# A new hand-searched order, nine check buffers and small operations shared with GpSimd in a three-stage fp32 kernel

## The chip, the cores and the metric

One Trainium2 chip, one core of it. Five engines of the core run their own instruction streams: TensorE (PE in the profile; PEld is its weight load, which runs beside the matmuls), VectorE (DVE), ScalarE (ACT), GpSimd (POOL) and SyncE (SP), which issues all data transfers (DMAs) of this kernel. The metric is the device time of one execution in microseconds (us), the median of several runs.

## The reference

The kernel computes three stages, in float32 with the weights of the two MoE stages given as float64 words:

```python
# attention: B=2, H=8, S=768, D=64; 8 global keys and a local window of 96
scores = q @ k.T / sqrt(D) - slope[h] * dist      # kept where (key < 8) or (0 <= row - key < 96)
a = softmax(scores); x = a @ v                    # x becomes [1536, 512]
# MoE 1: w_in [512, 2048], w_out [2048, 512]
h = x @ w_in
P = a[0] + a[1]*h + a[2]*h**2 + a[3]*h**3
Q = 1 + abs(b[0])*abs(h) + abs(b[1])*h**2
x = (P / (Q + 1e-6)) @ w_out
# MoE 2: w2_in [512, 1024], w2_out [1024, 512]
h = x @ w2_in
s = h * softmax(h)
out = ((s - mean(s)) / sqrt(var(s) + 1e-6) * g_ln) @ w2_out
```

## The kernel before

**Numbers.** Matmuls run on fp32r operands. Each operand is split into a high part (a cast) and a low part (the subtraction value - high, `minus`, L249), and each product is three matmuls: high by high, high by low, low by high. A weight tile comes in as 128x1024 32-bit words (the float64 pairs). The first loads use both words: L892, L896 and L900 on DVE put them together to 128x512 floats, L856/L858/L860 cast the high part (ACT, DVE or POOL) and L249 makes the low part (POOL, or DVE where the tile's number is in `WDVE`).

**Stages.** First, attention: 128-row tiles of queries, 64-wide heads, with PE L748/L751 for the scores, DVE L757 for mask, bias and maximum, ACT L765 for the exponential, PE L781 for the transposes and L788/L800 for the product with v. MoE 1 starts while attention still runs: 64 steps (four segments of 384 rows of x, the first of them done in two parts, by 16 slices of w_in), each with 12 matmuls L989, L991, L995, an elementwise chain on ACT and DVE (L1018 to L1038, of which L1021 is the step's first DVE reading of the matmuls' result and L1034, L1036, L1038 the later ones), and a split into g high and g low (L249 again, on DVE or POOL by the string `GLX`); then 12 matmuls L1086 or 9 of the 512-wide form L1088. MoE 2 has 12 tiles of 128 rows: 24 matmuls L1214 to L1216 (two halves of 512 columns), then the softmax and layer norm of `p2_soft` (DVE maximum L1236 and its negative L1237; ACT exponential L1261; DVE L1240 to L1243; ACT squares L1263; DVE variance L1247; ACT root L1250/1251; a Newton step of four 128x1 operations L1254 to L1257 and the scaling L1258 on DVE), transposes L1277 on PE with casts L1287 (lh) and low parts L249 (ll), 24 matmuls L1302 to L1304, a copy L1313 and the output DMA L1315.

**The weight check.** Words of float64 that are out of the fast path's range must be noticed. In the MoE 2 stage every weight tile is loaded a second time (48 loads of 512 KB, L959 on SP) into one of three buffers in the tile `t`, and DVE L957 ands its high words into `cv`. At the end `w_verdict` halves `cv` nine times (L967) and makes one number per row (L969 to L971), PE L1432 adds the rows, and DVE L224 to L229 turn it into the integer `fi`. All engines load `fi` (L1613); `tc.If` (L1614) then runs a slow path, which these inputs never take.

**What sets the order.** `record` (L557) lists some 2,100 operations, each with engine, modelled duration and the values it reads and writes. `Plan.follow` (L485) replays them in the order of the table `ORDER`, a permutation found by a search under the model; a tile of a pool goes to whichever operation comes next. Strings name the engine of each copy, cast or subtraction (A = ACT, D = DVE, P = POOL). Where the model sees PE idle for long, `fill` (L541) issues 128x128 matmuls on `warm` or `ident` (L544) into a free bank, whose result nobody reads.

```python
            if fill and e == "PE" and gap > (WARM[1] if t < WARM[0] else FILL[0]):
```

Of the kernel before, what the change touches and what calls it, by code (L numbers as in the profile page):

```python
# [1678 lines left out]
```

## Time and profile before

| | |
|---|---|
| time of three runs | 527.73, 529.74, 530.30 us; median 529.74 |
| the profiled execution | 534.36 us, its span 532.6 us |
| PE, PEld, DVE, ACT, POOL busy | 515.1, 448.0, 438.1, 324.3, 129.8 us |
| moved by DMA | 80.92 MB, 152 GB/s on average |

The span runs from the first to the last instruction of the profiled execution; 1.76 us of that execution lie outside it. The stretches of the span, by what PE works on: to about 24 us the start of attention with PE often waiting; to 48 us attention beside the first steps of MoE 1; to 204 us attention and MoE 1 together, ending at the L1021 of step 28; to 354 us MoE 1 alone; to 520 us MoE 2; the rest is the end. The row of a stretch gives each engine's busy time, the clock granted to TensorE (1.00 is 2.4 GHz, 0.50 is 1.2 GHz), the busy share of the DMA engines and what they moved.

### The profile page before, as it was taken

Reading aid. Unit: us, or ns where it says so; the run is one execution under the profiler, and the core shown is the slowest. Engines: PE = TensorE matmul, PEld = TensorE weight load, DVE = VectorE, ACT = ScalarE, POOL = GpSimd, SP = SyncE. Lnnn points to the kernel's source line nnn. Section 1 sums busy time; section 2 is a strip of 40 time slices with the busy share of each in tenths; the row PEclk is TensorE's granted clock in tenths of the full one; section 3 lists DMA queues with packets and bytes.
Section 4 is the critical chain, followed back from the end, with each engine's and each line's share of the span. In section 5 each row is a group of like instructions: output and inputs, shape, how many; then the busy total and the mean of one; then the engine's idle time right before and its main releaser. Section 6 shows DMA issues by size and latency. Waiting matters only on the chain.

```text
span 532.6 us, 9523 instructions
## 1 busy us (share of the span) xinstructions
PE 515.1 (97%) x3294; PEld 448.0 (84%) x3294; DVE 438.1 (82%) x1041; ACT 324.3 (61%) x751; POOL 129.8 (24%) x142
## 2 busy tenths in 40 slices
PE   8998989999999999999999999999999999999995
PEld 6776768887988878999999999998887888888885
DVE  4688999999898997967898999988779777879623
ACT  5577777887768698657666686667255342543310
POOL 3211335664534110013021124453333000000000
PEclk9998999999999999999999999999999999999998
DMA  6579765335672546300233224132344557778781
GB/s 193 172 221 306 237 205 168 124 107 158 197 231 68 164 145 192 92 0 1 69 106 108 90 75 128 42 104 95 118 139 156 165 180 234 240 232 246 263 258 50
DMA packets 37559, 80.92 MB, mean 152 GB/s; under 512 B 4864, under 2 KB 21504, under 8 KB 37504
## 3 DMA queue, kind: packets, MB, share of 16 engines
q1 hardware_dynamic: 37504, 80.24, 48.7%
q8 instruction: 28, 0.46, 0.4%
q14 instruction: 27, 0.22, 0.1%
HBM read 72.36 MB, written 7.86 MB: 151 GB/s over the span
## 4 chain that ended last, share of the span: by engine, by line
PE 58%; DVE 25%; ACT 6%; DMA 5%; issue 3%; SPq 1%; DVEq 0%; ACTq 0%
PE pb L1086 8%; PE pb L1088 5%; PE pb L1302 4%; PE pb L1303 4%; PE pb L1304 4%; PE pb L995 4%; PE pb L989 4%; PE pb L991 4%; PE pb L1214 3%; PE pb L1216 3%; PE pb L1215 3%; DVE cv L896 3%; DVE t L1034 3%; DVE t L1038 3%; PE pb L751 2%
## 5 line engine op out<-in xcount | busy, mean ns | idle before, releaser
L989 PE MATMUL pb<-x,w 128*128 128x384 f32 x256 | 88.3, 345 | 0.2
L991 PE MATMUL pb<-x,w 128*128 128x384 f32 x256 | 86.2, 337 | 0.0
L1088 PE MATMUL pb<-w,g 128*128 128x512 f32 x288 | 71.9, 398 | 0.6 <-DVE g L249 0.6
L1086 PE MATMUL pb<-g,w 128*128 128x384 f32 x384 | 69.8, 335 | 1.3 <-DVE g L249 1.3
L249 POOL TENSOR_TENSOR g<-t,g 128x384 fp32r<-128x384 f32 x37 | 41.0, 1112 | 122.1 <-ACT g L856 50.0
L1086 PEld LDWEIGHTS pb<-g,w 128*128 128x128 f32 x384 | 66.6, 188 | 2.4 <-DVE g L249 2.3
L1088 PEld LDWEIGHTS pb<-w,g 128*128 128x128 f32 x288 | 52.5, 188 | 12.4 <-DVE g L249 1.0
L249 POOL TENSOR_TENSOR w<-wst,w 128x512 fp32r<-128x512 f32 x35 | 47.9, 1374 | 38.5 <-ACT w L856 29.1
L995 PE MATMUL pb<-x,w 128*128 128x384 f32 x256 | 54.1, 337 | 0.0
L1020 ACT ACTIVATE t<-pb,poly 128x384 f32<-128x384 f32 x64 | 36.6, 579 | 24.0 <-PE pb L995 18.2
L1018 ACT ACTIVATE t<-pb,poly 128x384 f32<-128x384 f32 x64 | 42.3, 666 | 14.0 <-PE pb L995 10.2
L989 PEld LDWEIGHTS pb<-x,w 128*128 128x128 f32 x256 | 48.5, 190 | 2.4 <-DVE t L1021 0.8
L991 PEld LDWEIGHTS pb<-x,w 128*128 128x128 f32 x256 | 48.5, 190 | 0.1
L765 ACT ACTIVATE e<-e,st 128x192 f32<-128x192 f32 (+1 forms) x96 | 41.9, 439 | 8.7 <-DVE st L757 8.3
L995 PEld LDWEIGHTS pb<-x,w 128*128 128x128 f32 x256 | 44.9, 188 | 0.5 <-issue 0.3
L1021 DVE SCALAR_TENSOR_TENSOR t<-t,poly,pb 128x384 f32<-128x384 f32 x64 | 38.6, 606 | 6.6 <-ACT t L1018 3.3
L957 DVE SCALAR_TENSOR_TENSOR cv<-t,cv 128x512 int32<-128x512 int32 x47 | 32.7, 695 | 10.8 <-DMA t<-in_w_out 7.5
L1024 ACT ACTIVATE t<-t,poly 128x384 f32<-128x384 f32 x51 | 31.2, 614 | 14.2 <-DVE t L1036 6.7
L1302 PE MATMUL pb<-w,lh 128*128 128x512 f32 (+1 forms) x104 | 39.5, 380 | 0.2 <-ACT wst L1313 0.2
L1303 PE MATMUL pb<-w,lh 128*128 128x512 f32 (+1 forms) x104 | 39.1, 376 | 0.0
L1304 PE MATMUL pb<-w,ll 128*128 128x512 f32 (+1 forms) x104 | 38.8, 373 | 0.0
L1214 PE MATMUL pb<-w,yh 128*128 128x512 f32 x96 | 38.1, 397 | 0.0
(178 smaller groups left out, 1083.1 us busy)
## 6 DMA issues: line engine op xcount, KB each, us to landing
wst<-in_w_in SPq DMA_DIRECT2D x24, 512.0 KB, 4.2
wst<-in_w_out SPq DMA_DIRECT2D x24, 512.0 KB, 4.4
t<-in_w_in SPq DMA_DIRECT2D x24, 512.0 KB, 4.1
t<-in_w_out SPq DMA_DIRECT2D x24, 512.0 KB, 4.5
v<-in_qkv SPq DMA_DIRECT2D x80, 96.0 KB, 3.5
qk<-in_qkv SPq DMA_DIRECT2D x40, 192.0 KB, 3.2
out<-wst SPq DMA_DIRECT2D x11, 256.0 KB, 3.6
x_d<-x SPq DMA_DIRECT2D x2, 768.0 KB, 5.4
```

What stands on the lines that cost most here:

```text
L249: eng.tensor_tensor(out=out, in0=a, in1=hi.bitcast(F32), op=ALU.subtract)
L765: act.activation(out=x, in_=x, func=AF.Exp, scale=-1.0, bias=st[:, 0, c:c + 1], accum_out=st[:, 1, c:c + 1])
L989: pe.matmul(out=pb[:, g.h.slot, 0:n], lhsT=wt[wh.slot][:, cs[p]], rhs=xt[x[0].slot][:, p, 0:n], start=(p == 0), stop=False)
L991: pe.matmul(out=pb[:, g.h.slot, 0:n], lhsT=wt[wl.slot][:, cs[p]], rhs=xt[x[0].slot][:, p, 0:n], start=False, stop=False)
L995: pe.matmul(out=pb[:, g.h.slot, 0:n], lhsT=wt[wh.slot][:, cs[p]], rhs=xt[x[1].slot][:, p, 0:n], start=False, stop=(p == 3))
L1018: op("ACT", 0.2 + 0.467 * k, lambda: act.activation(out=T(g.c), in_=h(), func=AF.Square, scale=poly[:, 0:1], bias=poly[:, 1:2]), r=[g.h, v ...
L1086: pe.matmul(out=pb[:, y[i].slot, 0:n], lhsT=wt[w.slot][:, c], rhs=gt[a.slot][:, 0:n], **k)
L1088: pe.matmul(out=pb[:, y[i].slot, :], lhsT=gt[a.slot][:, c], rhs=wt[w.slot], **k)
L1214: pe.matmul(out=dst, lhsT=yh[:, m, :], rhs=wh, start=(m == 0), stop=False)
L1302: pe.matmul(out=pb[:, b.slot, c], lhsT=lh[:, f, :], rhs=wh[:, c], start=(f == 0), stop=False)
L1303: pe.matmul(out=pb[:, b.slot, c], lhsT=lh[:, f, :], rhs=wl[:, c], start=False, stop=False)
L1304: pe.matmul(out=pb[:, b.slot, c], lhsT=ll[:, f, :], rhs=wh[:, c], start=False, stop=(f == 7))
```

## The change

The table `ORDER` and all engine strings are new, found again by the search under a changed model: PE begins at 1.0 instead of 2.0 us, PE operations before 8 us are taken as 85% longer (`COLD`), and every transfer issued after 2 us as 0.9 us longer (`LATE`). Fillers before 8 us are 256 wide where two fit.

The x tiles of MoE 1 move to a pool of their own (`xp`). After their last use (`switch_x`) the space holds six more buffers for the weight check, so that loads go round over nine; loads into the six wait only for the weights' joins, no longer for the last g splits.

`w_verdict` has three instructions in place of twelve. In `p2_soft` the 128x1 operations become operations of their own, on DVE or POOL by `MNX`, `NGX`, `VRX`, `NWX`; on POOL the Newton step is six instructions. The two halves of the last output tile get a buffer each. `Flag.numbers` and `Flag.factors` take an engine (both stay on DVE), with three maxima in place of one reduction.

```diff
-GLX = 'DPPPPPPPPPDPDPPDPDDPDPDDPPPPDDDPPPDPDDPDDDDDDPPDDPPPDPDPPPPDPPDP'
+GLX = 'PPPPPPPPDPPPPPPPPPPDPPDDPDPDPPDDDDDPDPDDDPPDDDDDDDPDDPDPPDPPPDPD'
-YEX = "A" * 14
-XCX = "D" * 4
-WGX = "P" * 8
-XHX = "A" * 12
-YHX = "A" * 12
-LHX = "A" * 24
-OTX = "A" * 13
-WDVE = (7, 11, 18, 30, 31, 32, 34, 35, 36, 37, 38, 39, 43)
+YEX = 'AAAADADAAAADAD'
+XCX = 'AAPA'
+WGX = 'AAADDPAA'
+XHX = 'AAAAAAAAAAAD'
+YHX = 'DAADADAAAAAD'
+LHX = 'AAAADDAAADDADADAAADDDADA'
+OTX = 'AADDDAAAAAAAA'
+VRX = 'PPPPDPPDPDPD'
+NGX = 'DDDDDPDPDPPD'
+MNX = 'PDDPDDPDDPPD'
+NWX = 'PPPPDPPPPDPP'
+FLX = 'DD'
+WDVE = (4, 6, 9, 10, 20, 22, 23, 27, 28, 29, 30, 31, 32, 33, 34, 36, 39, 40, 41, 42, 43, 45, 47)
...
-BEGIN = {"PE": 2.0, "ACT": 2.5, "DVE": 1.0, "POOL": 1.0, "SP": 1.2, "X": 0.0}
+BEGIN = {"PE": 1.0, "ACT": 2.5, "DVE": 1.0, "POOL": 1.0, "SP": 1.2, "X": 0.0}
...
-                if idle <= BEGIN["PE"]:
-                    fill(int((gap + 1.0) / 0.5), spare, True)
+                if idle < COLD[0]:
+                    n = int((gap + WARM[2]) / 0.46)
+                    fill(n // 2, spare, 256)
+                    fill(n % 2, spare, 128)
...
-        st, first = Val("ck"), nseen[0] == 0
+        in_x, first = nseen[0] % 9 > 2, nseen[0] == 0
+        st = Val("ckx") if in_x else Val("ck")
...
-        w = 256
-        while w:
-            dve.tensor_tensor(out=a[:, 0:w], in0=a[:, 0:w], in1=a[:, w:2 * w], op=ALU.bitwise_and)
-            w //= 2
-        dve.tensor_scalar(out=a[:, 0:1], in0=a[:, 0:1], scalar1=0x78000000, scalar2=None, op0=ALU.bitwise_and)
-        dve.tensor_copy(bad, a[:, 0:1])
-        dve.tensor_scalar(out=bad, in0=bad, scalar1=float(0x78000000), scalar2=None, op0=ALU.not_equal)
+        dve.tensor_scalar(out=a, in0=a, scalar1=0x78000000, scalar2=None, op0=ALU.bitwise_and)
+        dve.tensor_reduce(out=bad, in_=a, op=ALU.min, axis=mybir.AxisListType.X)
+        dve.tensor_scalar(out=bad, in0=bad, scalar1=float(0x78000000), scalar2=None, op0=ALU.is_lt)
...
+    def switch_x():
+        held.pop(0).__exit__(None, None, None)
+        cm = tc.tile_pool(name="cp", bufs=1, side="right")
+        cp = cm.__enter__()
+        held.insert(0, cm)
+        bpt["ck"] = [cp.tile([128, 1024], I32, name=f"ck{i}") for i in range(6)]
...
+                pool.tensor_tensor(out=S(13), in0=S(12), in1=S(12), op=ALU.mult)
+                pool.tensor_tensor(out=S(13), in0=S(13), in1=S(11), op=ALU.mult)
+                pool.tensor_tensor(out=S(13), in0=S(13), in1=S(12), op=ALU.mult)
+                pool.tensor_scalar(out=S(13), in0=S(13), scalar1=-0.5, scalar2=None, op0=ALU.mult)
+                pool.tensor_scalar(out=S(12), in0=S(12), scalar1=1.5, scalar2=None, op0=ALU.mult)
+                pool.tensor_tensor(out=S(12), in0=S(12), in1=S(13), op=ALU.add)
```

DVE at the end of the program, before: the last look at the check's loads (L957), the verdict and the flag.

```order
L249 TENSOR_TENSOR ll_2746<-pb,lh_2744 128x512
L957 SCALAR_TENSOR_TENSOR cv<-t,cv 128x512 x6
L967 TENSOR_TENSOR cv<-cv 128x256
L967 TENSOR_TENSOR cv<-cv 128x128
...
L970 CAST bad<-cv 128x1
L971 TENSOR_SCALAR bad<-bad 128x1
L224 TENSOR_TENSOR fl<-fl,pb 128x1
L228 TENSOR_SCALAR fl<-fl 128x1
L229 CAST fi<-fl 128x1
```

DVE at the same place, after: L975 is the look at the check's loads, L983 to L985 the verdict, L1334 and L259 the last tile's lh and ll.

```order
L975 SCALAR_TENSOR_TENSOR cv<-t,cv 128x512
L983 TENSOR_SCALAR cv<-cv 128x512
L984 TENSOR_REDUCE bad<-cv 128x1
L985 TENSOR_SCALAR bad<-bad 128x1
L1334 CAST lh_2643<-pb 128x512
L216 TENSOR_TENSOR am<-coef 128x4
...
L259 TENSOR_TENSOR ll_2645<-pb,lh_2643 128x512 x2
L234 TENSOR_TENSOR fl<-fl,pb 128x1
L238 TENSOR_SCALAR fl<-fl 128x1
L239 CAST fi<-fl 128x1
```

The verdict stood behind the last tile's work on DVE and stands ahead of it now, with 19 operations of `factors` between the last cast and the last two low parts.

PE at the end, before (L1304 is the last output matmul, L544 the fillers, L1432 the count):

```order
L1303 MATMUL pb<-w_118,lh_2744 128x256
L1304 MATMUL pb<-w_119,ll_2746 128x256
L544 MATMUL pb<-ident 128x128 x26
L1432 MATMUL pb<-bad,t 128x1
L1613 TENSOR_LOAD fi
```

PE at the end, after:

```order
L1350 MATMUL pb<-w_127,lh_2643 128x256
L1351 MATMUL pb<-w_128,ll_2645 128x256
L1484 MATMUL pb<-bad,t 128x1
L1665 TENSOR_LOAD fi
```

The count now follows the last output matmul with no filler between them.

SP's queue at the end, before, with L959 the check's loads and L1315 the outputs:

```order
L1315 DMA out<-wst_157 128x512
L959 DMA t<-in_w_out 128x1024 x4
L1315 DMA out<-wst_155 128x256
L1315 DMA out<-wst_154 128x512
L1315 DMA out<-wst_155 128x256
```

SP's queue at the end, after:

```order
L1362 DMA out<-wst_161 128x512
L977 DMA t<-in_w_out 128x1024 x2
L1362 DMA out<-wst_164 128x512
L1362 DMA out<-wst_161 128x512
L1362 DMA out<-wst_163 128x512
L1362 DMA out<-wst_164 128x512
L1362 DMA out<-wst_161 128x256
L1362 DMA out<-wst_162 128x256
```

The last check load stood ahead of three outputs and stands ahead of six.

## Rows read from the trace of the kernel before

**Rows 1.** The page, first part: span, then busy time of each engine.

```profile
span 532.6 us, 9523 instructions
PE 515.1 (97%) x3294; PEld 448.0 (84%) x3294; DVE 438.1 (82%) x1041; ACT 324.3 (61%) x751; POOL 129.8 (24%) x142
```

**Rows 2.** Stretches: us, PE, PEld, DVE, ACT, POOL busy, PEclk, DMA share, GB/s.

```profile
0.00:24.00 24.00, 21.91 (x121) 16.79 (x123) 12.70 (x57) 12.29 (x44) 7.23 (x23) 1.00 0.62 182
24.00:48.00 24.00, 20.90 (x262) 15.82 (x262) 19.58 (x79) 18.01 (x57) 3.23 (x4) 1.00 0.83 242
48.00:51.50 3.50, 3.50 (x16) 3.07 (x15) 3.31 (x10) 3.18 (x12) 1.25 (x1) 0.51 0.99 356
51.50:125.00 73.50, 71.57 (x485) 59.87 (x484) 71.41 (x157) 56.52 (x129) 34.10 (x30) 1.00 0.57 177
125.00:204.00 79.00, 77.66 (x617) 64.34 (x616) 71.17 (x184) 63.32 (x168) 27.53 (x26) 1.00 0.53 156
204.00:354.00 150.00, 148.44 (x942) 143.71 (x941) 130.95 (x251) 102.17 (x204) 34.55 (x38) 1.00 0.27 81
354.00:520.00 166.00, 165.06 (x811) 138.40 (x810) 124.06 (x290) 68.18 (x140) 21.68 (x20) 1.00 0.60 189
520.00:532.60 12.60, 6.08 (x56) 5.99 (x54) 4.96 (x18) 0.65 (x2) 0.21 (x1) 0.87 0.14 50
```

**Rows 3.** The chain that ended last, by engine.

```profile
PE 58%; DVE 25%; ACT 6%; DMA 5%; issue 3%; SPq 1%; DVEq 0%; ACTq 0%
```

**Rows 4.** The waits of PE: waited for, total us, times, longest.

```profile
PE pb L751 <- DVE t L1021: 2.4, 3, 1.6
PE pb L1086 <- DVE g L249: 1.3, 2, 0.7
```

**Rows 5.** Timeline around a wait of attention's scores: start, duration, instruction.

```profile
47.82 0.70 PE L751 MATMUL pb<-qk 64*64 64x192 f32 x4 [1.59 <-DVE t L1021]
```

**Rows 6.** Timeline of the end.

```profile
519.87 0.28 PE L1304 MATMUL pb<-w,ll 128*128 128x256 f32 x1
519.99 5.97 PE L544 MATMUL pb<-ident 128*128 128x128 f32 x52
520.24 0.65 ACT L1313 COPY wst<-pb 128x256 f32<-128x256 f32 x2 [6.06 <-PE pb L1304]
520.63 1.31 SPq L1315 DMA_DIRECT2D out<-wst  x3
522.34 2.23 DVE L967 TENSOR_TENSOR cv<-cv 128x256 int32<-128x256 int32 x9
525.69 0.30 PEld L1432 LDWEIGHTS pb<-bad,t 128*128 128x128 f32 x2
526.49 0.15 DVE L229 CAST fi<-fl 128x1 int32<-128x1 f32 x1
```

**Rows 7.** DMA issues: count, KB each, median us from issue to landing.

```profile
out<-wst SPq DMA_DIRECT2D x2, 128.0 KB, 1.9
```

**Rows 8.** Groups by line: busy us, mean ns of one, idle before.

```profile
L249 POOL TENSOR_TENSOR w<-wst,w 128x512 fp32r<-128x512 f32 x35 | 47.9, 1374 | 38.5 <-ACT w L856 29.1 <-DVE w L858 8.9
L249 POOL TENSOR_TENSOR g<-t,g 128x384 fp32r<-128x384 f32 x37 | 41.0, 1112 | 122.1 <-ACT g L856 50.0 <-PE pb L1086 34.0 <-PE pb L991 11.5
L249 DVE TENSOR_TENSOR g<-t,g 128x384 fp32r<-128x384 f32 x27 | 15.6, 579 | 0.5 <-PE pb L1086 0.2
L1237 DVE TENSOR_SCALAR st<-st 128x1 f32<-128x1 f32 x12 | 1.8, 154 | 0.4
```

**Rows 9.** Timeline of a MoE 2 tile, from Newton step to transposes.

```profile
395.49 1.22 DVE L1255 SCALAR_TENSOR_TENSOR st<-st 128x1 f32<-128x1 f32 x1
397.12 0.81 DVE L1258 TENSOR_SCALAR wst<-wst,st 128x1024 f32<-128x1024 f32 x1
402.56 0.60 PE L1277 MATMUL pb<-ident,wst 128*128 128x128 f32 x4
```

**Rows 10.** Timeline of attention's first transposes.

```profile
13.12 1.11 PE L781 MATMUL pb<-ident,e 128*128 128x128 f32 x4
```

More of the change, by code (lines that the diff above doesn't have):

```diff
@@ L188, in __init__, with numbers @@
         self.fi = pool.tile([128, 1], I32, name="fi")
-    def numbers(self):
-        dve, nf, neg, nv, fl = self.nc.vector, self.nf, self.neg, self.nv, self.fl
+    def numbers(self, dve):
+        nf, neg, nv, fl = self.nf, self.neg, self.nv, self.fl
         dve.tensor_scalar(out=neg, in0=nf[:, :, 0], scalar1=0.0, scalar2=None, op0=ALU.is_lt)
@@ L200, in numbers, with factors @@
         dve.tensor_tensor(out=fl[:, 0:1], in0=fl[:, 0:1], in1=fl[:, 1:2], op=ALU.max)
-    def factors(self):
-        dve, coef, am, fl = self.nc.vector, self.coef, self.am, self.fl
+    def factors(self, dve):
+        coef, am, fl = self.coef, self.am, self.fl
         dve.tensor_tensor(out=am, in0=coef[:, 0:4], in1=coef[:, 0:4], op=ALU.mult)
-        dve.tensor_reduce(out=fl[:, 1:2], in_=am, op=ALU.max, axis=mybir.AxisListType.X)
+        for i in range(3):
+            dve.tensor_tensor(out=fl[:, 1:2], in0=fl[:, 1:2] if i else am[:, 0:1], in1=am[:, i + 1:i + 2], op=ALU.max)
         dve.tensor_tensor(out=fl[:, 1:2], in0=fl[:, 1:2], in1=am[:, 3:4], op=ALU.mult)
@@ L505, in follow @@
             if e == "PE":
-                wait, was = ENTER[was][o.cls], o.cls
+                wait, was = ENTER[was][o.cls] + (COLD[1] * o.occ if t < COLD[0] else 0.0), o.cls
             o.start, at[e], o.end = t, t + o.occ + wait, t + o.lat + wait
@@ L511, in follow @@
                 dma = max(dma, at[e]) + o.move
-                o.end = dma + o.lat
+                o.end = dma + o.lat + (LATE[1] if t > LATE[0] else 0.0)
             for v in o.vals:
@@ L538, in fast_path, with fill @@
     plan, held = record(tc, es, const, qkv, w_in, w_out, w2_in, w2_out, coef, ab2, g2, ident, flag, out)
-    def fill(n, spare, early=False):
+    def fill(n, spare, early=0):
         for _ in range(n if spare else 0):
-            x = warm if early else ident
-            nc.tensor.matmul(out=plan.pb[:, spare[0], 0:128], lhsT=x, rhs=x, start=True, stop=True)
+            o, x = plan.pb[:, spare[0], 0:max(early, 128)].rearrange("p (a c) -> p a c", c=128), warm if early else ident
+            o, r = bass.broadcast_tensor_aps(o, x.rearrange("p (a c) -> p a c", a=1))
+            nc.tensor.matmul(out=o, lhsT=x, rhs=r, start=True, stop=True)
     with tc.manual_schedule():
@@ L560, in record @@
     abt, ab, g_sb, g_ln = ab2[0], ab2[1], g2[0], g2[1]
+    xp_cm = tc.tile_pool(name="xp", bufs=1, side="right")
+    xp = xp_cm.__enter__()
+    xt = [xp.tile([128, 4, NMAX], F32R, name=f"x{i}") for i in range(4)]
     mp = es.enter_context(tc.tile_pool(name="mp", bufs=1))
@@ L574, in record @@
     gt = [mp.tile([128, NMAX], F32R, name=f"g{i}") for i in range(GB)]
-    xt = [mp.tile([128, 4, NMAX], F32R, name=f"x{i}") for i in range(4)]
     yt = [mp.tile([128, 512], F32, name=f"y{i}") for i in range(YB)]
@@ L587, in record @@
               "t": range(TB), "g": range(GB), "x": range(4), "y": range(YB), "qk": range(QB), "v": range(VB),
[L588 removed]
+              "e": range(EB), "st": range(3), "cv": [0], "ck": range(3), "ckx": range(6), "st2": range(3), "yh": [0, 1], "yl": [0, 1],
               "lh": [0, 1], "ll": [0, 1]})
@@ L949, in words @@
         def words():
+            if in_x:
+                return bpt["ck"][st.slot]
             return tall.rearrange("p a c -> p (a c)")[:, st.slot * 1024:st.slot * 1024 + 1024].bitcast(I32)
@@ L957, in seen @@
                 dve.scalar_tensor_tensor(out=a, in0=w1, scalar=0x40000000, in1=a, op0=ALU.bitwise_xor, op1=ALU.bitwise_and)
-        op("SP", 2.0, lambda: sync.dma_start(out=words(), in_=src.bitcast(I32)), occ=0.43, new=[st], move=2.1, after=gl[-4:] + joins[-1:], tag="ckl")
+        op("SP", 2.0, lambda: sync.dma_start(out=words(), in_=src.bitcast(I32)), occ=0.43, r=[vsx] if in_x else [], new=[st], move=2.1, after=joins[-1:] if in_x else gl[-4:] + joins[-1:], tag="ckl")
         op("DVE", 0.682, seen, r=[st], **{"new" if first else "w": [vacc]}, tag="ck")
@@ L1229, in E @@
         def E():
-            return wst[e.slot].bitcast(F32)
+            return wst[ev.slot].bitcast(F32)
         def S(a):
@@ L1236, in smax, with of, mneg @@
             dve.tensor_reduce(out=S(0), in_=H(), op=ALU.max, axis=mybir.AxisListType.X)
-            dve.tensor_scalar(out=S(2), in0=S(0), scalar1=-1.0, scalar2=None, op0=ALU.mult)
+        def of(x):
+            return "POOL" if x == "P" else "DVE", pool if x == "P" else dve
+        def mneg(eng):
+            eng.tensor_scalar(out=S(2), in0=S(0), scalar1=-1.0, scalar2=None, op0=ALU.mult)
         def times():
@@ L1242, in times, with neg, var @@
             dve.scalar_tensor_tensor(out=E(), in0=H(), scalar=S(6), in1=E(), op0=ALU.mult, op1=ALU.mult, accum_out=S(7))
-            dve.tensor_scalar(out=S(9), in0=S(7), scalar1=-1.0 / DFF2, scalar2=None, op0=ALU.mult)
-        def var():
-            dve.tensor_scalar(out=S(11), in0=S(10), scalar1=1.0 / DFF2, scalar2=1e-6, op0=ALU.mult, op1=ALU.add)
+        def neg(eng):
+            eng.tensor_scalar(out=S(9), in0=S(7), scalar1=-1.0 / DFF2, scalar2=None, op0=ALU.mult)
+        def var(eng):
+            eng.tensor_scalar(out=S(11), in0=S(10), scalar1=1.0 / DFF2, scalar2=1e-6, op0=ALU.mult, op1=ALU.add)
         def root():
@@ L1251, in root, with small @@
             act.activation(out=S(12), in_=S(12), func=AF.Exp, scale=-0.5)
+        def small(eng):
+            if eng is dve:
+                dve.tensor_tensor(out=S(13), in0=S(12), in1=S(12), op=ALU.mult)
+                dve.scalar_tensor_tensor(out=S(13), in0=S(13), scalar=S(11), in1=S(12), op0=ALU.mult, op1=ALU.mult)
+                dve.scalar_tensor_tensor(out=S(12), in0=S(12), scalar=3.0, in1=S(13), op0=ALU.mult, op1=ALU.subtract)
+                dve.tensor_scalar(out=S(12), in0=S(12), scalar1=0.5, scalar2=None, op0=ALU.mult)
+            else:
+                pool.tensor_tensor(out=S(13), in0=S(12), in1=S(12), op=ALU.mult)
[4 more added lines that the diff above has]
+                pool.tensor_tensor(out=S(12), in0=S(12), in1=S(13), op=ALU.add)
@@ L1253, in newton @@
         def newton():
-            dve.tensor_tensor(out=S(13), in0=S(12), in1=S(12), op=ALU.mult)
-            dve.scalar_tensor_tensor(out=S(13), in0=S(13), scalar=S(11), in1=S(12), op0=ALU.mult, op1=ALU.mult)
-            dve.scalar_tensor_tensor(out=S(12), in0=S(12), scalar=3.0, in1=S(13), op0=ALU.mult, op1=ALU.subtract)
-            dve.tensor_scalar(out=S(12), in0=S(12), scalar1=0.5, scalar2=None, op0=ALU.mult)
             dve.tensor_scalar(out=E(), in0=E(), scalar1=S(9), scalar2=S(12), op0=ALU.add, op1=ALU.mult)
-        op("DVE", 1.407, smax, r=o.h, new=[st], tag="max2")
@@ L1261, in p2_soft @@
-        op("ACT", 1.205, lambda: act.activation(out=E(), in_=H(), func=AF.Exp, bias=S(2), accum_out=S(3)), r=o.h, w=[st], new=[e], tag="exp2")
-        op("DVE", 1.86, times, r=o.h, w=[st, e], tag="times")
-        op("ACT", 1.245, lambda: act.activation(out=H(), in_=E(), func=AF.Square, bias=S(9), accum_out=S(10)), r=[e], w=o.h + [st], tag="sq2")
-        op("DVE", 0.15, var, w=[st], tag="var")
+        k = o.k
+        op("DVE", 1.25, smax, r=o.h, new=[st], tag="max2")
+        e, n = of(MNX[k])
@@ new lines, in p2_soft @@
+        op(e, 0.2 if n is pool else 0.15, lambda n=n: mneg(n), w=[st], tag="mneg" if n is dve else "mnegP")
+        op("ACT", 1.205, lambda: act.activation(out=E(), in_=H(), func=AF.Exp, bias=S(2), accum_out=S(3)), r=o.h, w=[st], new=[ev], tag="exp2")
+        op("DVE", 1.7, times, r=o.h, w=[st, ev], tag="times")
+        e, n = of(NGX[k])
+        op(e, 0.2 if n is pool else 0.15, lambda n=n: neg(n), w=[st], tag="neg" if n is dve else "negP")
+        op("ACT", 1.245, lambda: act.activation(out=H(), in_=E(), func=AF.Square, bias=S(9), accum_out=S(10)), r=[ev], w=o.h + [st], tag="sq2")
@@ L1265, in p2_soft @@
+        e, n = of(VRX[k])
+        op(e, 0.2 if n is pool else 0.15, lambda n=n: var(n), w=[st], tag="var" if n is dve else "varP")
         op("ACT", 0.437, root, w=[st], tag="root")
-        op("DVE", 1.642, newton, w=[st, e], tag="newton")
+        e, n = of(NWX[k])
+        op(e, 1.2 if n is pool else 0.83, lambda n=n: small(n), w=[st], tag="nws" if n is dve else "nwsP")
+        op("DVE", 0.82, newton, r=[st], w=[ev], tag="newton")
     def p2_tr(o):
@@ L1295, in p2_o @@
         w = 512 // n
-        b, ot = Val("y2"), Val("wst", "ot")
+        b, ots = Val("y2"), [Val("wst", "ot") for _ in range(n)]
         def mm(c):
@@ L1309, in p2_o @@
                     **{"w" if i else "new": [b]}, occ=5.505 / n + (0.13 if n > 1 else 0.0), tag="o") for i, c in enumerate(cs)]
-        for i, c in enumerate(cs):
+        for i, (c, ot) in enumerate(zip(cs, ots)):
             e = OTX[o.k + i]
             copy = act.copy if e == "A" else dve.tensor_copy
-            op("ACT" if e == "A" else "DVE", (0.585 if n == 1 else 0.372) + (0.0 if e == "A" else 0.1), lambda c=c, copy=copy: copy(wst[ot.slot].bitcast(F32)[:, c], pb[:, b.slot, c]), r=[b],
-               **{"w" if i else "new": [ot]}, tag="ot" if e == "A" else "otD")
-            op("SP", 2.0, lambda c=c: sync.dma_start(out=out[rows, c], in_=wst[ot.slot].bitcast(F32)[:, c]), occ=0.4, r=[ot], move=1.0, tag="out")
+            op("ACT" if e == "A" else "DVE", (0.585 if n == 1 else 0.372) + (0.0 if e == "A" else 0.1), lambda c=c, copy=copy, ot=ot: copy(wst[ot.slot].bitcast(F32)[:, c], pb[:, b.slot, c]), r=[b],
+               new=[ot], tag="ot" if e == "A" else "otD")
+            op("SP", 2.0, lambda c=c, ot=ot: sync.dma_start(out=out[rows, c], in_=wst[ot.slot].bitcast(F32)[:, c]), occ=0.4, r=[ot], move=1.0, tag="out")
     steps = [(si, f) for si, (j, f0, f1) in enumerate(SEGS) for f in range(f0, f1)]
@@ L1410, in record @@
             made2 += 1
+    op("X", 0.0, switch_x, w=[vsx], after=[o for o in P.ops if any(v.pool == "x" for v in o.vals)])
     vflag = Val()
@@ L1422, in record @@
         if k in (6, 8):
-            part_, d = (flag.numbers, 1.38) if k == 6 else (flag.factors, 3.43)
-            op("DVE", d, part_, r=[vnn, vpoly], w=[vflag], after=[fr[k].op], tag="flag")
+            part_, d = (flag.numbers, 1.38) if k == 6 else (flag.factors, 3.45)
+            x = FLX[k // 8]
+            op("POOL" if x == "P" else "DVE", d * (1.3 if x == "P" else 1.0), lambda part_=part_, x=x: part_(pool if x == "P" else dve), r=[vnn, vpoly], w=[vflag],
+               after=[fr[k].op], tag="flP" if x == "P" else "fl")
+            if not wide and k == 8:
+                op("DVE", 0.3, flag.integer, w=[vflag], tag="flag")
         if wide and 1 <= k <= 8:
@@ L1429, in record @@
             bank = Val("h")
-            op("DVE", 2.8, w_verdict, w=[vacc, vbad], tag="flag")
+            op("DVE", 1.3, w_verdict, w=[vacc, vbad], tag="flag")
             op("POOL", 0.3, lambda: pool.memset(ones, 1.0), r=[vacc], w=[vones], tag="ck")
```

23 lines of the change are left out of this document (12 added, 11 removed), and 157 rows, old and new, of the table ORDER.

## The prediction, made before the changed kernel ran

> **What bounds the kernel now.** I read the busy shares first: PE is busy 515.1 of 532.6 us, DVE 438.1, and no other engine comes near [rows 1]. The chain of waits agrees: 58% of it is PE and 25% DVE [rows 3]. PE's work for the three stages is the same in both kernels (only fillers differ), so a gain has to come from time in which PE stands still, runs filler, or runs at the lower clock. The table of stretches shows where that is [rows 2]. Idle time is the length less the busy time: 2.09 us in 0 to 24, 3.10 in 24 to 48, 1.93 in 51.5 to 125, 1.34 in 125 to 204, 1.56 in 204 to 354 and 0.94 in 354 to 520. From 24 to 520 that is 8.87 us in 496. At 48 to 51.5 the granted clock is 0.51, the lower of its two levels; what came before is a stop of PE for 1.59 us at attention's scores, which wait for DVE's L1021 [rows 5]. With 3.50 us at half rate some 1.7 us are lost there. PE's own waits name DVE: 2.4 us at L751 and 1.3 us at L1086 [rows 4]. In the last stretch PE is busy 6.08 of 12.6 us, but nearly all of that is filler. So three places are open: the start, the 8.87 + 1.7 us in between, and the end.
>
> **The end.** The last output matmul is done at 519.87 + 0.28 = 520.15, which I call T. DVE then ends the check and its verdict, PE counts, and DVE writes the flag: its last instruction ends at 526.49 + 0.15 = 526.64, so T + 6.49; from there to the span's end are 5.96 us in which every engine loads the flag and the program closes [rows 6]. In the new order the verdict stands ahead of the last tile's lh and ll on DVE, and the count stands behind the last output matmul with no filler between them. The verdict's shortening from twelve instructions to three thus saves nothing by itself: it lies beside PE's matmuls anyway. What is left behind T is from the count's weight load to the flag, 525.69 to 526.64: 0.95 us [rows 6]. That saves 6.49 - 0.95 = 5.5 us.
>
> Against it stand the outputs. The last copies end at 520.24 + 0.65 = 520.89, T + 0.74; three issues on SP took 1.31, so 0.44 each, and an output of 128 KB lands 1.9 us after its issue [rows 6, 7]. The last one lands at about T + 0.74 + 0.44 + 1.9 = T + 3.1. Before, it was down long ahead of the flag; now it is later than the flag's T + 0.95. If the closing waits for it from its start, the gain is 6.49 - 3.1 = 3.4 us. If the 5.96 us hide it, 5.5. I take 5.2, near the second, since the landing's 2.15 us beyond the flag are less than half of the 5.96. In SP's queue six outputs now stand behind the last check load instead of three; a load takes its issue only, so I give them nothing.
>
> The last 19 operations of `factors` now stand on DVE between the last cast and the last low parts. At 0.154 each [rows 8] they are 2.9 us; they run where DVE is 75% busy (124.06 of 166) [rows 2], and low parts feed the output matmuls only after the transposes. I cost them at nothing; if they come late, up to 2.9 us.
>
> **The order between.** The new order can win at most the 8.87 us of stops and the 1.7 at half clock, and it can lose. I can't replay it, so I counted instructions on DVE by step of MoE 1 and gave each the mean of its line. Up to the L1021 of step 28 (204 us) the sums differ by no more than half a us at any step. From there to the L1021 of step 60 DVE has 22 more instructions of 128x384 or wider (among them 5 g low parts, 3 scalings of y, 2 g_ln scalings; 4 casts of x are gone): by the 0.579 of a g low part on DVE [rows 8], 12.7 us more. DVE is busy 130.95 of 150 us there [rows 2], so it fits in the 19.05 us left, with 6.3 to spare. In return POOL loses work that takes it 1.112 or 1.374 us each [rows 8], about twice as long, and low parts come sooner to PE. I take a net gain of 1.5 us for everything between 24 and 520 us: the stop at 48 us with its half clock is worth 1.59 + 1.7 and a new order has some chance to lose it. Ends: 7 us gained (two thirds of 10.6), 6 lost (below).
>
> **The 128x1 operations of MoE 2.** Of 36 single ones 17 go to POOL, and ten Newton steps become six POOL instructions each. No 128x1 instruction of POOL stands in the trace. The two POOL rows are 1.374 us for 512 elements and 1.112 for 384 [rows 8]; the line through them gives 0.33 us at none. The bounds are 0.154 (as on DVE) and 1.112 each. I take 0.33: six are 2.0 us, against four on DVE that take 0.154 each when nothing disturbs them, so a Newton step is 1.4 us later, at most 6 x 1.112 - 0.62 = 6.1 us. In the tightest tile the scaling ends at 397.12 + 0.81 = 397.93 and the transposes that need it start at 402.56, 4.63 us later [rows 9]. So 1.4 is hidden, and the upper bound would stop PE by 1.5 us in one tile. I take 0. DVE is relieved of 57 instructions there, some 9 us, which PE doesn't wait for: its idle is 0.94 in that stretch.
>
> **The check's nine buffers.** DVE's look at the loads (L957) is beside PE's matmuls; more buffers let loads go ahead, and what they compete with are MoE 2's few other transfers, at a DMA share of 0.60 [rows 2]. I take 0; it is a condition of the early verdict, though, and priced there.
>
> **The start.** Fillers and the planned begin change what PE does in the first 14 us. The four transposes at 13.12 take 1.11 us, where the same four at 402.56 take 0.60 [rows 9, 10]: half rate, though the stretch's granted clock reads 1.00. If the new fillers don't change this, 0. Ends: 5 us gained, 1 lost.
>
> **Sum.** 5.2 + 1.5 = 6.7 us. The profiled execution is 534.36 us (534.36 - 532.6 = 1.76 lie outside the span), so 527.7 for a like one. The median is 529.74, 4.6 below the profiled one; I take the same 6.7 off it: 523.0.
>
> **Rivals.**
>
> *The clock rises earlier.* The start's transposes at half rate speak for work in the first 14 us that runs at twice its time. PE is busy 21.91 of 24 us there, much of it filler, so half rate costs only where PE is the one waited for; against it, loads decide much of this stretch. If half of the first 13 us' work is real and runs at full rate, some 3 to 4 us more: 519. The Trainium skill, "TensorE: Matmul & The Clock Gate", Part 1, says that the array starts with its clock gated and that its own activity releases it; the transposes' 1.11 against 0.60 agrees, and by that rule wider fillers could bring the release forward.
>
> *DVE becomes the bound in MoE 1, and the outputs hold the end.* With 143.65 of 150 us, DVE would be at 96%. In 51.5 to 125 it is at 97% (71.41 of 73.5) and PE idles 2.6% of the time [rows 2]; 2.6% of 150 is 3.9 us against 1.56, so 2.4 us lost. With an end that gains only 3.4 the sum is 1.0: 528.7. For it speaks that DVE's 128x1 L1255 took 1.22 us instead of some 0.16 while POOL had a w low part [rows 9]: work beside POOL gets longer. The Trainium skill, "SBUF — State Buffer", section "SBUF: two separate sides", has DVE and GpSimd share one pair of ports that whoever starts first holds for the whole instruction; the 1.22 us agrees, and by that rule the 77 instructions new on POOL stretch DVE's in MoE 2. PE waits there for neither, so the sum stays.
>
> *The verdict is late all the same.* If the last check load comes late, the verdict still ends behind T. Three instructions instead of twelve save then about 2.23 + 0.45 - 1.2 = 1.5 us [rows 6] (0.45 for three single numbers at 0.15; 1.2 is my estimate for the new three, two passes over 512 words near the 0.579 of rows 8): 528.2. Against it: in the order the loads end six outputs before the end.
>
> *Loads hold PE in attention: slower.* In 24 to 48 us PE idles 3.10 of 24 us, 13%, at a DMA share of 0.83; after that the share is 0.57 and PE idles 2.6% [rows 2]. An order planned with longer transfers issues loads in another sequence; if scores and v come late and weights early, the 13% spreads over 51.5 to 125. 13% of 73.5 is 9.5 against 1.93, so 7.6 us lost, and another 1.7 for a second drop of the clock, less 5.2 at the end: 4.1 slower, 533.8. It decides from 7.9 us of new stops. Against it: the planner charges transfers more than before, which should move loads ahead.
>
> **How the numbers follow.** 0.5% of the median is 2.65 us, about what a measurement can tell from no change: 527.09 to 532.39 is "same". Forecast 523.0 with its own ends 520 to 526.5 (from 3.4 instead of 5.2 at the end and no gain between, to 3 more between): 0.56. Clock earlier, 519: 0.20. DVE bound, 528.7: 0.12. Verdict late, 528.2: 0.05. Loads, 533.8: 0.07. Faster: 0.56 + 0.20 and 0.02 of the edge cases, 0.78. Same: 0.15. Slower: 0.07. The range 516 to 529 takes in the start's bound below and DVE's case above, and leaves out the loads.
>
> **What would show it.** The end: from the last output matmul to the flag's cast about 1 us, no filler there, and the three verdict instructions ahead of T. Between: idle of PE from 24 to 520 us near 7, and no stretch at 0.51. MoE 2: POOL's 128x1 at about 0.33 us and transposes without a wait for L1297. DVE in the MoE 1 part near 144 of 150 us with PE idle under 2. Start: the first four transposes at 1.1 us still. I am wrong if PE waits for DVE or loads by several us more in any stretch, if the closing grows by the outputs' landing, or if PE's first 24 us shrink.

## The result and the profile after

The changed kernel takes 515.24 us, the median of four runs (514.79 to 515.84), beside 529.23 for the kernel before (527.73 to 530.30): a ratio of 0.974, interval 0.971 to 0.977. That is 14.0 us faster, where 6.7 were forecast; 515.24 lies 0.8 below the range. The profiled execution is 514.79 us, its span 512.7.

Busy times and the chain that ended last, of the changed kernel; they answer to [rows 1, 3].

```profile
span 512.7 us, 9400 instructions
PE 499.0 (97%) x3236; PEld 435.5 (85%) x3236; DVE 439.3 (86%) x1012; ACT 318.5 (62%) x740; POOL 129.5 (25%) x193
...
PE 78%; DVE 9%; DMA 4%; ACT 3%; issue 3%; POOL 1%; SPq 1%; DVEq 0%; ACTq 0%; POOLq 0%
```

DVE's work is the same 439 us as before (438.1) in 20 us less, and its share of the chain fell from 25% to 9%. The stretches of the changed kernel, cut where the work corresponds to [rows 2] (columns: us, PE, PEld, DVE, ACT, POOL busy, PEclk, DMA share, GB/s):

```profile
0.00:24.00 24.00, 21.73 (x208) 15.89 (x208) 18.06 (x81) 17.07 (x65) 3.50 (x19) 1.00 0.75 220
24.00:48.00 24.00, 22.08 (x209) 17.68 (x206) 21.50 (x74) 20.06 (x57) 6.94 (x6) 1.00 0.86 267
48.00:125.00 77.00, 76.00 (x536) 64.67 (x534) 75.17 (x177) 63.76 (x152) 41.45 (x38) 1.00 0.61 195
125.00:190.00 65.00, 64.98 (x540) 54.92 (x539) 61.91 (x163) 51.86 (x138) 15.96 (x15) 1.00 0.49 139
190.00:338.00 148.00, 147.67 (x942) 143.88 (x941) 133.78 (x264) 104.33 (x208) 26.58 (x27) 1.00 0.31 93
338.00:505.00 167.00, 165.78 (x808) 137.75 (x807) 128.38 (x255) 60.78 (x124) 35.07 (x89) 1.00 0.55 185
505.00:512.70 7.70, 0.77 (x8) 0.68 (x6) 0.47 (x3) 0.65 (x2) 0.00 (x0) 0.84 0.14 45
```

From 24 to 505 us PE idles 1.92 + 1.00 + 0.02 + 0.33 + 1.22 = 4.5 us (before 8.87), and no stretch has a clock of 0.51. In the first 24 us it does 208 instructions in place of 121, most of them at the higher clock. The transposes of the start take 0.66 us for four, where [rows 10] have 1.11:

```profile
10.54 0.66 PE L796 MATMUL pb<-ident,e 128*128 128x128 f32 x4
```

The longest waits of PE, to set beside [rows 4]: it waits for transfers now, and for DVE's L1035 (L1021 before) or a low part of g no longer by a row of its own.

```profile
PE pb L815 <- DMA v<-in_qkv: 2.0, 2, 1.5
PE pb L557 <- DVE coef L1661: 1.1, 1, 1.1
PE pb L796 <- DVE st L772: 0.8, 1, 0.8
```

The wait for DVE is not gone for good, though. In a second profile of the changed kernel (e15 below, 517.57 us) it is back, and PE idles 2.99 of 77 us from 48 to 125 instead of 1.00, with DVE as busy as here (75.16):

```profile
PE pb L766 <- DVE t L1035: 1.9, 1, 1.9
```

The end, to set beside [rows 6]:

```profile
505.37 0.28 PE L1351 MATMUL pb<-w,ll 128*128 128x256 f32 x1
505.49 0.28 PE L1484 MATMUL pb<-bad,t 128*128 128x1 f32 x2
505.69 0.65 ACT L1360 COPY wst<-pb 128x256 f32<-128x256 f32 x2 [6.01 <-PE pb L1351]
506.18 0.15 DVE L239 CAST fi<-fl 128x1 int32<-128x1 f32 x1
```

The last output matmul ends at 505.65, the flag is ready at 506.33, the span ends 7.08 us behind that matmul. Before, it was 12.42 in the profile as read and 12.92 in another (e13).

**When the clock rises.** The column PEclk reads 1.00 for time ahead of the clock's first record, so it hid what the traces' clock records tell. These are all of them, in us from the span's start (e1 to e18 are the experiments below):

```
                     up at   later at half rate
before               24.19   48.08-51.49
e13 (before again)    5.45   8.86-15.69
e14 (before again)   20.63   -
e1  (before's order)  5.71   9.13-15.95
e6  (before's order)  4.25   31.55-34.97
after                 5.06   -
e2 e3 e4 e7 e8 e12 e15 e17 e18 (after's fillers)  4.51 to 6.51   -
e9                    4.97   11.79-18.62
e10                   6.54   371.77-375.18
e11                   3.87   10.70-14.11
e16                   6.37   -
e5 (no early fillers) 24.48  -
```

(Each trace also ends in a stretch at half rate, left out here.) With the kernel before, the moment differs from run to run; its times lie between 523.2 and 535.3 us over the runs beside the experiments. The one that I read in [rows 1 to 10], 534.36, had a late one. With the changed kernel's fillers it was up by 6.54 us in all 14 profiles.

**Where the 14 us are.** I summed PE's matmuls, fillers left out, each at the length that its form has at the full clock. That sum is the work done, and the table says how much later a kernel had begun the same amount of it. The kernel before stands three times: as read, and e13 and e14. Single entries move by about 1 us with where the cut falls; the last column does not.

```
work done, us               20    50    60    80   160   280   360   all
before (534.36) - after    5.9   7.9  10.9  10.9  14.3  15.0  15.7  14.5
e13    (528.83) - after    3.3   2.6   5.5   5.5   8.2   8.9   9.6   8.4
e14    (532.41) - after    5.2   5.4   8.9   8.8  12.2  12.7  13.4  12.2
```

e13 is close to the medians of before. Against it the start gives 3.3 us, the order of attention and MoE 1 (from 20 to 360 us of work) 6.3, the rest takes back 1.2, and behind the last output matmul 12.92 - 7.08 = 5.8 are saved: together 14.2. The 1.2 is mostly the overlap of the two MoE stages: counted from the last matmul of MoE 1 (364.28 here, 373.00 in e13) MoE 2 takes back 0.3. Of the 5.1 us between start and end, PE's idle time explains 2.8 (7.25 us in e13 from 24 us to the last output matmul, 4.49 here). The other 2.3 lie in gaps between matmuls that the busy time covers, since a matmul's end is modelled; what they wait for is not shown.

### The profile page after: what moved, and what is told of

The parts are those of the page before. It is cut to its first block, busy times and chain, and to the rows that moved or that the text cites. A ratio compares the mean times of both kernels' runs of the same rounds, so it can differ in the third digit from the quotient of the medians.

```text
span 512.7 us, 9400 instructions
## 1 busy us (share of the span) xinstructions
PE 499.0 (97%) x3236; PEld 435.5 (85%) x3236; DVE 439.3 (86%) x1012; ACT 318.5 (62%) x740; POOL 129.5 (25%) x193
## 4 chain that ended last, share of the span: by engine, by line
PE 78%; DVE 9%; DMA 4%; ACT 3%; issue 3%; POOL 1%; SPq 1%; DVEq 0%; ACTq 0%; POOLq 0%
PE pb L1100 12%; PE pb L1102 9%; PE pb L1003 8%; PE pb L1005 8%; PE pb L1009 8%; PE pb L1349 3%; PE pb L1350 3%; PE pb L1351 3%; PE pb L1237 3%; PE pb L1239 3%; PE pb L1238 3%; PE pb L766 3%; PE pb L815 3%; PE pb L796 3%; PE pb L1324 2%
## 5 line engine op out<-in xcount | busy, mean ns | idle before, releaser
L259 POOL TENSOR_TENSOR g<-t,g 128x384 fp32r<-128x384 f32 x36 | 41.5, 1158 | 142.5 <-PE pb L1100 72.5
L259 POOL TENSOR_TENSOR w<-wst,w 128x512 fp32r<-128x512 f32 x25 | 33.5, 1345 | 68.4 <-ACT w L871 31.2
L1034 ACT ACTIVATE t<-pb,poly 128x384 f32<-128x384 f32 x64 | 36.5, 577 | 14.5 <-PE pb L1009 8.1
L1035 DVE SCALAR_TENSOR_TENSOR t<-t,poly,pb 128x384 f32<-128x384 f32 x64 | 38.7, 608 | 7.0 <-ACT t L1032 6.1
L1237 PE MATMUL pb<-w,yh 128*128 128x512 f32 x96 | 38.3, 399 | 0.1
L1239 PE MATMUL pb<-w,yl 128*128 128x512 f32 x96 | 37.6, 391 | 0.0
L1238 PE MATMUL pb<-w,yh 128*128 128x512 f32 x96 | 37.5, 390 | 0.0
```

What stands on the lines that cost most here:

```text
L259: eng.tensor_tensor(out=out, in0=a, in1=hi.bitcast(F32), op=ALU.subtract)
L1237: pe.matmul(out=dst, lhsT=yh[:, m, :], rhs=wh, start=(m == 0), stop=False)
L1238: pe.matmul(out=dst, lhsT=yh[:, m, :], rhs=wl, start=False, stop=False)
L1239: pe.matmul(out=dst, lhsT=yl[:, m, :], rhs=wh, start=False, stop=(m == 3))
```

## The experiments

All are variants of the changed kernel unless it says otherwise; times are medians.

**Fillers at the start: e1, e2, e5, e6.** e1, in the kernel before, and e2, the other way round:

```diff
-                    fill(int((gap + 1.0) / 0.5), spare, True)
+                    n = int((gap + 1.0) / 0.5)
+                    fill(n // 2, spare, 256)
+                    fill(n % 2, spare, 128)
```

> The kernel before with its early fillers 256 wide, half as many of them (the same columns), nothing else changed. Theory A (the fillers' shape sets when the clock first rises): the clock's first record comes near 5 us instead of 24.2, the work up to 24 us is done some 6 us sooner, and the time falls from 529.2 to about 523. Theory B (what raises the clock is the new order: scores without the wait of 1.04 us, more columns): the clock rises at about 24 us as before, 529.2 within 1 us.

> The changed kernel with its early fillers 128 wide, twice as many (the same columns). Theory A: the clock rises late again, near 20 to 24 us, and the time grows from 515.2 by 5 to 7 us, to about 521. Theory B: the clock rises near 5 us, 515.2 within 1 us.

e1 took 529.4 us beside 529.6 for the kernel before (ratio 1.002, interval 0.998 to 1.007), e2 515.0. The fillers' width is worth nothing in time, and theory A falls. (e1's one trace has the clock up at 5.71, as theory A had it, and down again from 9.13; but the unchanged kernel does the same in e13.)

e5 takes the early fillers out (`pass` in place of `fill`); e6, in the kernel before, doubles those ahead of the third scores matmuls (`2 * int((gap + 0.15) / 0.5)` before 7 us).

> The changed kernel without any of its early fillers. If fillers (of either width) are what keeps PE at work until the clock rises, it now rises near 24 us or later as in the profile of the kernel before, and the time grows by 5 to 7 us, to about 521. If the new order's real work alone raises it, the clock rises within the first 10 us and the time stays at 515.2 within 1.5 us.

> The kernel before with six early fillers instead of three ahead of the third scores matmuls, where PE stood still for 1.04 us waiting for a load. Theory B1 (that stop is what keeps the clock down, or lets it fall again, in the first 24 us): the clock rises near 5 us and stays, the median falls from 529.5 to about 525 with a smaller scatter between runs. Theory B2 (the stops of the later order, at 46 us and after, matter as much): less than 2 us.

e5 took 518.9, 3.6 more, the clock of its one trace up at 24.48. Real work alone does not raise it early there, and the same transposes are at half rate again:

```profile
11.41 1.11 PE L794 MATMUL pb<-ident,e 128*128 128x128 f32 x4
```

That trace has begun 20 us of work 5.1 us later than the changed kernel, about as late as the kernel before as read (5.9): by this one trace the start's gain is the clock, not the order.

e6 took 526.9 beside 528.3 (ratio 0.996, interval 0.993 to 0.999), a gain of less than 2 us as theory B2 has it; its ten times scatter less, 523.8 to 528.0 beside 524.5 to 531.9. Its clock was up at 4.25, ahead of the place that I had filled, and the stop of PE there was still 1.36 us, since fillers at the higher clock take half as long (12 records 1.60 us there, 6 records 1.65 in the profile as read). So its trace does not test whether this stop keeps the clock down. In e13 and e1 a stop of 1.82 and 1.96 us at the same place stands just ahead of the fall at 8.86 and 9.13; in e15 a stop of 1.93 us, at 50 us, brings no fall. Why one run of the kernel before rises at 5 us and another at 20 or 24 stays open, and so does what makes the rise early in every profile of the changed kernel with its fillers, since the kernel before has early fillers too.

**The end: e3, e11, e16, e12.** e3 puts the 26 fillers back; e11 moves the count and the flag ahead of the last tile's output matmuls in `ORDER`, and e16 is e11 again, beside the changed kernel again (e15).

```diff
+                for _ in range(26):
+                    pe.matmul(out=pb[:, bank.slot, 0:128], lhsT=ident, rhs=ident, start=True, stop=True)
...
-2145, 2138, 2139, 2150, 2151, 2148, 2154, 2152, 2149,
+2145, 2148, 2149, 2138, 2139, 2150, 2151, 2154, 2152,
```

> The changed kernel with the 26 fillers of 128x128 between the last output matmul and the count, as before the change. If the count and the flag are the path behind the last matmul, the fillers' 52 records at 0.115 us add their 6.0 us: 521.2. If the outputs' landing, some 3 us behind the last matmul, holds the end of the changed kernel, 2.4 us of that are hidden: 518.8.

> The changed kernel with the count matmul and the flag's three DVE instructions moved ahead of the last tile's output matmuls; the flag is then ready before the last output matmul, 505.65. If the flag (0.68 us behind that matmul) is what the closing starts from, the span gets 0.7 us or more shorter: 514.0 to 514.6. If the outputs' landing holds the closing, nothing: 515.2 within 0.3.

> The changed kernel with the count and the flag ahead of the last output matmuls. The trace of its first run had 6.20 us from the last output matmul to the span's end where the changed kernel has 7.08: 0.9 us less than the changed kernel in the same call, 514.2. If the gain of the first timing was scatter, the same time within 0.3 us.

> The changed kernel again: clock up between 4 and 7 us as in all ten profiles with its fillers so far, 515 us.

e3 took 521.3, 6.0 more, and its span ends 12.95 us behind the last output matmul, 5.87 more than 7.08: the fillers stood wholly on the path, and no landing hid a part. e11 took 514.3 and e16 514.3 (513.4 to 515.5) beside 515.6 for e15 (514.6 to 518.0). From the last output matmul to the end e11 has 6.20 and e16 6.03, e15 7.11. That is 0.9 to 1.1 us by the traces; the two sets of times overlap, so the times alone would not show it. The flag of e16:

```profile
500.47 0.15 DVE L239 CAST fi<-fl 128x1 int32<-128x1 f32 x1
...
506.30 0.28 PE L1351 MATMUL pb<-w,ll 128*128 128x256 f32 x1
506.61 0.65 ACT L1360 COPY wst<-pb 128x256 f32<-128x256 f32 x2 [6.01 <-PE pb L1351]
```

It is ready 6 us ahead of the last matmul, and the end came only 7.11 - 6.03 = 1.1 us nearer. What holds the last 6.03 us (the outputs, or the closing itself) was not tried.

e12 puts the twelve instructions of the verdict back.

> The changed kernel with the verdict's twelve instructions of before in place of three. Prediction's step (beside PE's matmuls, nothing by itself): 515.2 within 0.5 us. Rival (its 1.5 us more on DVE make the last low parts late): up to 1.5 more, 516.7.

514.9: the verdict's length is worth nothing. Its place was not moved back in a run. In the kernel before the verdict's last instruction was

```profile
524.99 0.15 DVE L971 TENSOR_SCALAR bad<-bad 128x1 f32<-128x1 f32 x1
```

and the fillers ended at 519.99 + 5.97 = 525.96 [rows 6], later than it, as in the four other profiles of that order. So the fillers held the count, and an early verdict gains nothing while they stand: e3's end of 12.95 us is as long as e13's of 12.92. Without them the late verdict would have held the count instead; its end lay 2.4 to 5.0 us behind the last output matmul in these five profiles. The plan sets the fillers where its model has PE wait for the verdict, so the early verdict is also what took them away.

**The 128x1 operations: e4.** `VRX`, `NGX`, `MNX` and `NWX` become `'D' * 12`.

> The changed kernel with all 128x1 operations of MoE 2 on DVE (57 instructions back, 77 fewer on POOL), the same order. The prediction's step (PE doesn't wait for them): 515.2 within 1 us. The rival (their 9 us on DVE come back as waits of PE for the low parts ll): 517 to 520.

518.7: 3.5 us more, of which the span has 2.5 (the rest lies outside the span, and nothing here shows why). PE's longest wait in its MoE 2, which the changed kernel doesn't have there:

```profile
PE pb L1237 <- ACT pb L1307: 2.5, 3, 1.1
```

PE doesn't wait for low parts but for a bank: L1237 of the next tile needs the one that ACT's squares L1307 free. That these come later because DVE's steps ahead of them do is my reading; the views show only that they wait for DVE's L1273. POOL's durations of such operations are near the 0.33 that I had taken:

```profile
L1289 POOL TENSOR_TENSOR st<-st 128x1 f32<-128x1 f32 x10 | 3.4, 340 | 27.1 <-ACT st L1280 27.1
L1294 POOL TENSOR_TENSOR st<-st 128x1 f32<-128x1 f32 x10 | 1.9, 195 | 0.8
L1265 POOL TENSOR_SCALAR st<-st 128x1 f32<-128x1 f32 x5 | 1.8, 362 | 28.4 <-DVE st L1259 19.1 <-DVE st L1268 9.3
```

**Nine buffers: e7, e17.** `in_x` is False, and a load goes out as soon as one of three buffers is free; e17 also leaves out the fillers that the plan sets after 14 us.

> The changed kernel with three buffers for the weight check instead of nine; DVE's order is unchanged, a check load goes out as soon as one of the three buffers is free. If the nine buffers matter (prediction: only as the condition of the early verdict), DVE's looks at the loads wait some us each, the low parts behind them come late to PE, and the time grows by more than 5 us. If they don't, 515.2 within 1 us.

> The changed kernel with three check buffers (as e7) and without the fillers that the plan sets after the first 14 us. If the loss of e7 is waits of PE for low parts that stand behind a look at a late load, the time stays near 526; if it is the fillers themselves, it falls to 516 to 519.

e7 took 526.5, 11.3 more, but the plan had set 104 filler records into it. Without them e17 took 518.6: 3.3 us are the buffers' own, the other 8 were fillers that took longer than the waits they filled. From the last matmul of MoE 1 to the last output matmul e17 falls back by 3.0 us. DVE's looks wait for loads 14.5 us (the changed kernel: 3.2), and the low parts behind them come late. PE's transposes (L1340) wait 1.4 of the 3.0 us for them, needing banks that these low parts read; waits of DVE, then of PE, in e17:

```profile
DVE cv L991 <- DMA t<-in_w_in: 9.4, 9, 2.3
DVE cv L991 <- DMA t<-in_w_out: 5.1, 5, 1.7
...
PE pb L1340 <- DVE ll L259: 1.4, 3, 0.6
```

**Who makes the low parts: e8, e9, e10, e18.** The strings of the kernel before in the new order: GLX and WDVE (e8), GLX alone (e9), WDVE alone (e10), both without late fillers (e18).

```diff
-WDVE = (4, 6, 9, 10, 20, 22, 23, 27, 28, 29, 30, 31, 32, 33, 34, 36, 39, 40, 41, 42, 43, 45, 47)
+WDVE = (7, 11, 18, 30, 31, 32, 34, 35, 36, 37, 38, 39, 43)
```

> The changed kernel with the strings GLX and WDVE of the kernel before: the low parts of w and g are made by DVE and POOL as they were (11 fewer on DVE, 11 more on POOL), in the new order. If the shift of low parts to DVE is what took PE's waits for them away, PE waits for POOL's low parts and the time grows by 2 to 5 us. If only the order counts, within 1 us.

> The changed kernel with the string GLX alone of the kernel before (which engine makes each low part of g: 27 on DVE instead of 28, but other ones). If the places of the g low parts carry the 11.7 us that both strings together cost, about 523 to 526; if WDVE carries them, 515.2 to 517.

> The changed kernel with WDVE alone of the kernel before (13 low parts of weights on DVE instead of 23, ten more on POOL at 1.35 us each). If POOL's slower low parts are what PE waited for, 520 to 526; if GLX carries the loss, 515.2 to 517.

> The changed kernel with the old GLX and WDVE (as e8) and without those fillers. If PE waits for the low parts, the time stays at 524 to 527; if the 32 more filler records (3.7 us at 0.115) were pure cost, about 523; if they were all of it, 515.

e8 took 526.9, e9 521.1, e10 525.2, e18 527.0: 11.7, 5.8, 9.9 and 11.7 more than the changed kernel. Here the waits are real, not filler. In e18 PE idles 3.72, 2.50 and 2.33 us in

```profile
48.00:125.00 77.00, 73.28 (x508) 60.59 (x506) 75.93 (x165) 60.53 (x140) 39.33 (x36) 1.00 0.60 186
125.00:200.00 75.00, 72.50 (x593) 61.26 (x591) 69.96 (x177) 57.99 (x154) 21.62 (x20) 1.00 0.47 139
200.00:350.00 150.00, 147.67 (x932) 143.34 (x929) 133.16 (x258) 103.57 (x206) 33.90 (x33) 1.00 0.29 90
```

in a dozen stops of 0.3 to 1.2 us. Few of them are put down to a low part itself; the longest in all of e18, and the two on low parts of g:

```profile
PE pb L766 <- DVE st L772: 2.0, 3, 1.2
...
PE pb L1102 <- POOL g L259: 0.9, 1, 0.9
PE pb L1100 <- DVE g L259: 0.9, 1, 0.9
```

The rest stand behind other steps of DVE and ACT and behind transfers. That the moved low parts delay those is argued, not shown. DVE's share from 48 to 125 us is the same as in the changed kernel (75.93 and 75.17 of 77). A low part of w takes 1.345 us on POOL and 0.729 on DVE:

```profile
L259 POOL TENSOR_TENSOR w<-wst,w 128x512 fp32r<-128x512 f32 x25 | 33.5, 1345 | 68.4 <-ACT w L871 31.2 <-DVE st L831 21.4 <-PE pb L1100 8.1
...
L259 DVE TENSOR_TENSOR w<-wst,w 128x512 fp32r<-128x512 f32 x23 | 16.8, 729 | 0.0
```

So the new order is only worth its gain with the low parts on the engines that it was searched with; the other strings were not tried by themselves. It does not follow that the old order would gain 10 us from the new strings; that was not tried.

**The kernel before, twice more: e13, e14.**

> The kernel before, unchanged, one more profile. If the moment of the clock's first rise is a matter of the run, it comes near 4 to 6 us or near 24 us, and a run with an early rise takes about 524 to 528 us; if this order always raises it late, near 24 us again and about 530.

> The same kernel a third time, with the same two readings: run to run, another moment than in the two other profiles; always late, near 24 us.

528.83 with the clock up at 5.45 (and down again from 8.86 to 15.69), 532.41 with 20.63: run to run.

## Why the prediction was right or wrong

The direction was right, the size half of what came: of the 7.5 us missing against e13, 3.6 are the order between, 3.3 the start and 0.6 the end. By its steps:

**The end** was right in mechanism and near in size: 5.2 taken, 12.42 - 7.08 = 5.34 measured against the profile as read, 5.8 against e13. The flag came 0.69 us behind the last output matmul instead of the 0.95 taken. From the flag to the end it is 6.39 us; the 5.96 of the profile as read were the low end of a scatter (6.42 in e13, 6.30 in e14), so the outputs' landing, for which 0.3 was taken off, cost nothing that shows. e3 shows the path; e12 that the shortened verdict saves nothing.

**The order between** is the first of two steps that failed, a term of the sum that was too small: 1.5 us taken for 24 to 520 us, 5.1 measured (6.3 in attention and MoE 1 less 1.2 behind them) even against e13, whose clock stayed up from 15.69 us on, 7.0 against e14 and 8.6 against the profile as read. I had named the place, the 8.87 us of stops and the drop at 48 us, and put them at the low end because DVE gets more work. That count was a poor brake. DVE's share from 48 to 125 us is 97.6% where it was 97%, and PE's idle there fell to 1.00 of 77 us where [rows 2] have 1.93 of 73.5 (but 2.99 in e15, at the same share). In MoE 1 alone, between the L1035 of steps 28 and 60 (the old L1021; 186.69 to 339.15), DVE is busy 138.24 of 152.46 us: 7.3 more than [rows 2] and not the 12.7 that I counted, 91% and not the 96% that I feared. PE idles 0.33 us there. What PE waits for is one result at a time; e8 to e10 and e18 show that which engine makes a low part, and when, is worth up to 11.7 us at the same share of DVE. Which places of the order gave the 5.1 us stays open: half of it doesn't show as idle time at all. The end of 7 us gained, which I had written, would have held what e13 and e14 show, not the 8.6. The 6 lost at the other end have no sum behind them; the rival of the loads makes it 7.6 + 1.7.

**The start** is the second: it was taken as nothing, on the condition that the new fillers change nothing there, and gave 3.3 us against e13 and 5.9 against the profile as read. It was my first rival, with 519 as its time. Its reason was right in kind (half rate up to 24 us) but not that wider fillers do it (e1, e2); in the new order fillers of either width do (e2, e5), and in the old one neither did reliably. I had seen the half rate at 13 us but took it for the first 14 us alone, since the row reads 1.00; that reading has no record behind it. The Trainium skill, "TensorE: Matmul & The Clock Gate", Part 1, has the array's own activity release the gate; e5 agrees in that fillers bring the rise from 24.48 to some 5 us. But the profile of before stayed at half rate up to 24.19 with PE busy all the time from 8 us on, as two of its stretches show:

```profile
8.00:12.00 4.00, 4.00 (x20) 3.33 (x20) 2.17 (x11) 2.49 (x12) 0.26 (x1) 1.00 0.65 216
...
16.00:20.00 4.00, 4.00 (x29) 2.47 (x29) 2.04 (x10) 2.27 (x11) 0.00 (x0) 1.00 0.54 166
```

So the busy share of the profile does not tell when the clock rises.

**The 128x1 operations on POOL** were taken as nothing, and MoE 2 as a whole gave nothing against the order before (0.3 lost); their duration was right (0.20 to 0.36). But DVE's relief was not worth nothing: in the new order it is 2.5 us of the span (e4). **The nine buffers** were taken as nothing and are worth 3.3 in the new order (e17). They are not a condition of the early verdict, as I had it: with three the verdict still ends at 499.46, 10.3 us ahead of the last output matmul. I count neither as a term of its own, since by e4 and e17 both only keep the order's gain.

**The rivals.** DVE as the bound with the landing at the end: neither happened. The L1255 of 1.22 us that spoke for it usually takes 0.22 and not some 0.16. The verdict late: it ended at 492.4, 13 us early. Loads that hold PE: PE idles 1.92 us at 24 to 48 and 1.00 up to 125. The sum was made on a profile of 534.36 us with a late rise and taken off a median of 529.74; the 5.9 us of the start in that profile are 3.3 against e13, whose 528.83 is nearer to that median.

## What to carry to other kernels

Where a search places instructions, count what the bounding engine waits for and not how busy the other is: with DVE at 97 to 98%, PE stopped for 1.9 us in one order, and for 1.0 in one run and 3.0 in another run of the next. A view that reads full clock before its first record proves nothing; look at the same instruction early and late. One profile of each kernel is not enough to split a gain of this size. And what ends behind the last useful matmul is the surest term of such a sum: here it came within 0.1 to 0.6 us of the estimate.
